# Attention statistics in PSUM, sums beside the values, and seven products in the second FFN throughout

## The chip, the cores and the metric

The kernel runs on one core of one Trainium2 chip. Its engines each work through an instruction queue of their own, in order: TensorE (PE; its weight loads are listed as PEld), VectorE (DVE), ScalarE (ACT), GpSimd (POOL) and SyncE (SP), which issues the DMAs. PE, DVE and ACT reach both on-chip memories, SBUF and PSUM; PE writes its results to PSUM, which is handled here as eight banks of 128 x 512 floats. The metric is the device time of one execution in microseconds (us). The profile is that of one execution.

## The reference

```python
xn = _layernorm(x)                                   # 2048 tokens x 512
qkv = xn @ wqkv                                      # 32 heads of 16
pq, pk = q @ w_phi, k @ w_phi                        # per head, 16 x 16
phi = concatenate([softmax(p), softmax(-p)])         # 32 features per head
kv = einsum("bhsf,bhsd->bhfd", phi_k, v)
z  = einsum("bhsf->bhf", phi_k)
num = einsum("bhqf,bhfd->bhqd", phi_q, kv)
den = einsum("bhqf,bhf->bhq", phi_q, z)[..., None] + 1e-6
s = (num / den).reshape(B, S, D) @ wo
act = mish(xn @ w1 + b1)                             # 1792 wide
g = silu(act @ w2)
return x + s * g
```

## The kernel before

Tokens are worked in 16 tiles of 128 (NT) or 4 groups of 512 (NG); the hidden width of 1792 is worked in 7 blocks of 256 (NB). A float32 factor is split in a high part (ACT rounds it) and a low part (DVE or POOL subtracts), and a product of two factors is three PE products, low x high, high x low, high x high. Most of the large products are of 128 x 128 weights with 512 columns.

Two by two block products are often done by seven products instead of eight (the schemes Ka to Kd for keys and values, Fa to Fd for the first FFN, Ga, Gb, Gc with Gd or Ge and Gf for the second). In the second FFN a unit is one group of 512 tokens and one block. Units of token groups 0 and 1 are plain (parts G0 to G13: 24 PE products each); groups 2 and 3 go as pairs by seven products (Ga7 to Ga13 and so on: 42 PE products for a pair and a block).

The attention runs in parts. K and Ka to Kd give keys and values; `k_soft` makes the features of a key tile: maximum and minimum per head, two subtractions to e, exponential on ACT, sum, reciprocal, scaling. `q_soft` (S) loads the projected queries qp, which had been written to DRAM as qd, and does the same without the scaling. `kv_acc` (A0 to A7) multiplies features with values into one PSUM bank, kvp, for two tiles at a time, and adds the features of all tokens in SBUF, zacc. `sums` (z) turns kvp and zacc into kvw, through DRAM, and the row sums zb, by four PE products pz with ones. `den` (D0 to D15) multiplies a query tile with zb (ez), sums to tz, takes the reciprocal, scales the tile and transposes it to ph. `num` (U) computes the numerators pn, `att_out` (O0 to O15) multiplies with wo (pw) and puts the result so in DRAM. `final` (E) reads it back, applies silu and adds x.

What runs where and when is set by three tables. ORDER lists the parts. SCHED lists every single operation of all parts in the order of issue, and for an operation that can go to two engines (`either`: DVE or POOL; `copy`: ACT or DVE) the letter behind the number (V, G, A) picks the engine. PLACE lists the buffer of each tile in its pool (slot, s2, sm, rq, st, tq, and ps for PSUM). Since queues run in order, an instruction that waits holds up all behind it on its engine.

All instructions of the loop are recorded by one helper, `call`, so their line is L184 in the profile; the names of the tiles tell them apart.

Of the kernel before, what the change touches and what calls it, by code (L numbers as in the profile page):

```python
# [37 lines left out]
Fa11 Fc10 Fc7 Fd10 D4 P5 P6 S5 Fd7 Fb11 Fc11 Fa13 D5 Fb13 Fa12 S7 S8 Fc13 Fb12 Fc12 Fd13 D8 D6 L2 S9 Fd11 Fa4 Fb4 S13
wo0 D7 Fd12 Fa5 Fc4 D9 Fa6 Fb6 Fc6 Fb5 Fd6 R0 Fc5 wo1 U1 Fd4 R2 Fd5 U0 G0 D10 O7 O4 O0 S11 D11 O3 S12 O2 D12 D13 S14
O6 O1 T0 R1 O5 B1 R3 G1 G2 G3 D14 R4 T1 R6 G4 R5 G5 G6 E3 Ga7 Ga8 S15 D15 G7 Ga9 E2 G8 T2 Ga10 E1 G9 E0 G10 G11 T4  # L40
Ga11 G12 G13 Ga12 Ga13 E7 E6 U3 Gb7 U2 Gb8 E5 O13 E4 O11 T3 Gb9 O8 Gb10 O14 B3 Gb11 O15 B0 B2 B4 Gb12 T6 B5 Gb13 O9 B6
E8 Gc7 O12 Gc8 Gc9 Gc10 Gc11 Gc12 Gc13 Ge7 Ge8 E9 Ge9 Ge10 O10 Ge11 Ge12 E14 E15 E12 E13 Ge13 Gf7 Gf8 E10 Gf9 Gf10
Gf11 Gf12 Gf13 E11
"""
SCHED = """
# [884 lines left out]
```

## Time and profile before

| | |
|---|---|
| median of 3 runs | 490.1 us (489.66 to 490.27) |
| span of the profiled execution | 488.0 us (its own time is not listed apart) |
| start of the first PE product | 1.1 us |
| end of the last PE product | 482.7 us |
| POOL, 128 x 1024 products ez of one tile | 2.4 us |
| DMAs on SP's queue, to and from HBM | 115.55 MB, mean 237 GB/s |

A row of a group reads: line, engine, operation, tile written <- tiles read, shapes, count | busy us, mean ns of one | idle time of the engine before them and what ended it. A row of waits reads: engine, tile, line <- what was waited for: us in total, times, longest. A row of the chain or of the timeline begins with start and length in us. PE's row lengths overlap, since products are pipelined; their cost in a stream is read from start to start or from the chain.

### The profile page before, as it was taken

The page shows a single profiled execution, that of the slowest core. Times are in us where ns is not written, and L with a number is a line of the kernel's source. Part 1 is how long each engine was busy: PE and PEld are TensorE (multiplying, and loading weights), DVE is VectorE, ACT ScalarE, POOL GpSimd, SP SyncE. Part 2 cuts the span into 40 slices and gives each one's busy share as a digit, 9 for nine tenths or more (in the row PEclk, how much of TensorE's full clock was granted, in tenths as well). Part 3 has the DMA queues.
Part 4 walks back from the last instruction along what each step waited for, and adds up shares of the span by engine and source line. Part 5 has one row for each costly group of instructions (what it writes and reads, how often), then busy time and mean ns, then how long its engine had stood idle before and what let it go on. Part 6 is the DMA issues. An engine that isn't in the chain of part 4 may idle for free.

```text
span 488.0 us, 8581 instructions
## 1 busy us (share of the span) xinstructions
PE 481.5 (99%) x3122; PEld 397.9 (82%) x3122; DVE 429.3 (88%) x687; ACT 284.6 (58%) x447; POOL 244.5 (50%) x188
## 2 busy tenths in 40 slices
PE   9999999999999999999999999999999999999995
PEld 9888888888888888888888878888888887888884
DVE  5989898899999997999999989998678588879984
ACT  5998777235154504325434676598976677576721
POOL 2675859967335786686557963312622032412021
PEclk9999999999999999999999999999999999999999
DMA  8956649165686789879969979788486615468543
GB/s 303 346 169 233 245 173 365 69 192 198 207 289 223 234 294 303 303 213 357 333 214 283 363 242 332 239 274 279 167 262 217 230 56 163 152 210 284 168 147 140
DMA packets 65594, 115.55 MB, mean 237 GB/s; under 512 B 7056, under 2 KB 32016, under 8 KB 65552
## 3 DMA queue, kind: packets, MB, share of 16 engines
q1 hardware_dynamic: 65408, 114.98, 69.9%
q8 instruction: 24, 0.39, 0.3%
q14 instruction: 18, 0.15, 0.1%
q10 hardware_dynamic: 144, 0.03, 0.0%
HBM read 72.92 MB, written 42.07 MB: 236 GB/s over the span
## 4 chain that ended last, share of the span: by engine, by line
PE 99%; DVE 0%; ACT 0%; DVEq 0%; issue 0%; ACTq 0%
PE y L184 20%; PE fx L184 16%; PE q L184 9%; PE pw L184 9%; PE kx L184 8%; PE x L184 8%; PE fy L184 8%; PE ky L184 4%; PE fz L184 4%; PE pn L184 2%; PE kz L184 2%; PE z L184 2%; PE kvp L184 2%; PE pt L184 1%; PE v L184 1%; PE k L184 1%
## 5 line engine op out<-in xcount | busy, mean ns | idle before, releaser
L184 PE MATMUL q<-wqh,xT 128*128 128x512 f32 x128 | 42.3, 393 | 0.0
L184 ACT ACTIVATE r<-r,b1t 128x512 f32<-128x512 f32 x56 | 38.1, 719 | 1.2 <-DMA r<-hd 1.1
L184 PEld LDWEIGHTS q<-wqh,xT 128*128 128x128 f32 x128 | 24.0, 188 | 5.0
L184 PE MATMUL q<-wql,xT 128*128 128x512 f32 x64 | 24.9, 390 | 0.0
L184 ACT ACTIVATE hc<-fx 128x512 f32<-128x512 f32 x11 | 6.5, 599 | 26.8 <-PE fx L184 15.9
L184 ACT ACT_TABLE_LOAD x16 | 20.5, 1283 | 0.3
L184 POOL TENSOR_TENSOR rs<-rs,mhalf 128x1 f32<-128x1 f32 x16 | 9.7, 615 | 19.7 <-DVE rs L184 19.7
L184 DVE TENSOR_REDUCE tz<-ez 128x64 f32<-128x1024 f32 x16 | 19.2, 1206 | 0.1
L184 PE MATMUL kx<-wss,th 128*128 128x512 f32 x56 | 17.3, 390 | 0.0
L184 POOL TENSOR_TENSOR tl<-ts,th 128x1024 fp32r<-128x1024 f32 x6 | 14.4, 2407 | 4.5 <-ACT th L184 3.1
L184 DVE TENSOR_TENSOR ol<-pn,oh 128x256 fp32r<-128x256 f32 x32 | 11.9, 416 | 5.1 <-ACT oh L184 5.1
L184 POOL TENSOR_TENSOR w1al<-w1a,w1ah 128x768 fp32r<-128x768 f32 x4 | 8.2, 2046 | 14.2 <-DVE w1sl L184 9.2
L184 POOL TENSOR_TENSOR w<-w2r,w 128x512 fp32r<-128x512 f32 x7 | 9.9, 1428 | 9.3 <-ACT w L184 9.3
L184 ACT ACTIVATE qs<-q 128x512 f32<-128x512 f32 x15 | 8.7, 594 | 9.4 <-PE q L184 5.0
L184 PEld LDWEIGHTS q<-wql,xT 128*128 128x128 f32 x64 | 12.0, 188 | 2.4
L184 ACT ACTIVATE oh<-pn 128x256 fp32r<-128x256 f32 x32 | 10.7, 393 | 4.9 <-PE pn L184 3.6
L184 POOL TENSOR_TENSOR w1s<-w1a 128x256 f32<-128x256 f32 x9 | 8.9, 995 | 7.4 <-PE q L184 7.1
L184 PE MATMUL pw<-oh,wo0l 128*128 128x512 f32 x32 | 12.4, 389 | 0.0
L184 PE MATMUL pw<-ol,wo0h 128*128 128x512 f32 x32 | 12.4, 389 | 0.0
L184 PE MATMUL pw<-oh,wo0h 128*128 128x512 f32 x32 | 12.4, 389 | 0.0
L184 PE MATMUL pw<-oh,wo1l 128*128 128x512 f32 x32 | 12.4, 389 | 0.0
L184 PE MATMUL pw<-ol,wo1h 128*128 128x512 f32 x32 | 12.4, 389 | 0.0
(869 smaller groups left out, 1833.1 us busy)
## 6 DMA issues: line engine op xcount, KB each, us to landing
r<-hd SPq DMA_DIRECT2D x28, 512.0 KB, 5.0
x<-x SPq DMA_DIRECT2D x16, 256.0 KB, 6.1
scr<-xT SPq DMA_DIRECT2D x8, 512.0 KB, 5.1
scrT<-th SPq DMA_DIRECT2D x8, 512.0 KB, 3.5
qd<-qs SPq DMA_DIRECT2D x16, 256.0 KB, 4.6
scrT<-tl SPq DMA_DIRECT2D x8, 512.0 KB, 4.8
qp<-qd SPq DMA_DIRECT2D x16, 256.0 KB, 5.1
xx<-xt SPq DMA_DIRECT2D x16, 256.0 KB, 4.9
```

What stands on the lines that cost most here:

```text
L184: getattr(g, m)(*a, **k)
```

## The change

- `softmax` keeps maximum, minimum, sum and (for keys) reciprocal in a PSUM bank `st` (tiles k0m, q0m and so on) of 6 x 32 columns instead of three SBUF tiles. Both subtractions and the scaling are fixed on DVE. The same holds for the small steps of `den`, all in a bank tz; the fused step (scalar_tensor_tensor) becomes a reduce and an addition of 1e-6.
- A value tile v has a last row of 16 ones (`v_tile`). `kv_acc` uses the values and these ones as weights' partner: the features e of a head are 32 weight columns, and the 16 values with the 16 ones are the 32 moving columns, so kvp holds the sums of keys times values and, beside them, the row sums. 32 products a tile instead of 16, each of 32 columns instead of 64. zacc, the ones_r products pz and the way of kvw through DRAM (5 DMAs) go.
- Queries are loaded by four DMAs of 64 KB a tile, in an order by which a plain 32 x 32 block transposition gives ph. `num` works on 4 tiles a time: 32 products of 512 columns instead of 64 of 256 (4 units as before), and the split of its result is 16 pairs of 512 columns instead of 32 of 256.
- The second FFN goes by seven products for all token groups; `ffn2` (the plain units) is gone. The pieces of w2 are loaded and split apart (`prep2`: R, `prep2d`: C, `prep2a`: T, `prep2b`: B, by `pair2`), for four blocks the sums of w2 lie in the pool tq.
- The final gate works in a PSUM bank, its two products fixed on DVE. b1 comes transposed from the host.
- ORDER, SCHED and PLACE are new throughout; the helper's line is L190.

Instructions before and after: PE matmul 2567 to 2649 (second FFN -42, numerators -128, kvp +256, pz -4); DVE tensor_tensor 383 to 407, reduce 112 to 128, tensor_scalar 63 to 81, scalar_tensor_tensor 16 to 0; POOL tensor_tensor 179 to 171; ACT activation 406 to 421; DMAs on SP 320 to 370.

```diff
+POOLS = dict(slot=SLOTS, s2=S2, tq=2, sm=13, rq=RQ, st=48, ps=8)
...
-Ga11 G12 G13 Ga12 Ga13 E7 E6 U3 Gb7 U2 Gb8 E5 O13 E4 O11 T3 Gb9 O8 Gb10 O14 B3 Gb11 O15 B0 B2 B4 Gb12 T6 B5 Gb13 O9 B6
+Gb2 O11 T3 Gb3 T4 Gb4 T5 O8 Gb5 T6 Gb6 B0 Gc0 O14 B1 Gc1 B2 Gc2 B3 Gc3 O15 B4 Gc4 B5
...
-    def softmax(p, name, r):
+    def softmax(p, name, r=None):
         p3 = p.rearrange("p (h d) -> p h d", d=DH)
-        mm = sm([P, 2, H], name + "m")
-        V.tensor_reduce(mm[:, 0, :], p3, axis=X, op=ALU.max)
-        V.tensor_reduce(mm[:, 1, :], p3, axis=X, op=ALU.min)
+        st = bank([P, 6, H], name + "m")
+        V.tensor_reduce(st[:, 0, :], p3, axis=X, op=ALU.max)
+        V.tensor_reduce(st[:, 1, :], p3, axis=X, op=ALU.min)
         e = slot([P, H, 2, DH], name + "e")
-        hi, lo = (mm[:, i, :, None].to_broadcast([P, H, DH]) for i in range(2))
-        either(e[:, :, 0, :], p3, hi, op=ALU.subtract)
-        either(e[:, :, 1, :], lo, p3, op=ALU.subtract)
+        hi, lo = (st[:, i, :, None].to_broadcast([P, H, DH]) for i in range(2))
+        V.tensor_tensor(e[:, :, 0, :], p3, hi, op=ALU.subtract)
+        V.tensor_tensor(e[:, :, 1, :], lo, p3, op=ALU.subtract)
         A.activation(e, e, AF.Exp)
-        s = sm([P, 2 * H], name + "s")
+        s = st[:, 2:4].rearrange("p a h -> p (a h)")
         V.tensor_reduce(s, e.rearrange("p h s d -> p (h s) d"), axis=X, op=ALU.add)
+        if r is None:
+            r = st[:, 4:6].rearrange("p a h -> p (a h)")
         V.reciprocal(r, s)
-        return e
+        return e, r
 
     def scale(e, r):
         e2 = e.rearrange("p h s d -> p (h s) d")
-        either(e2, e2, r[:, :, None].to_broadcast([P, 2 * H, DH]), op=ALU.mult)
-
-    kvp = bank([P, 4, 64], "kvp")
-    zacc = slot([P, 2 * D], "zacc")
+        V.tensor_tensor(e2, e2, r[:, :, None].to_broadcast([P, 2 * H, DH]), op=ALU.mult)
+
+    kvp = bank([P, 8, 32], "kvp")
...
+    def v_tile(t):
+        v = alloc("s2", [P, H + 1, DH], f"v{t}")
+        vp[t] = v
+        copy(v[:, H], ones[:, 0:DH])
+        return v[:, 0:H].rearrange("p h d -> p (h d)")
...
     def q_soft(t):
         p = s2(f"qp{t}")
-        Q.dma_start(p, qd[t])
+        for c in range(4):
+            Q.dma_start(p[32 * c:32 * c + 32, :].rearrange("p (b f) -> p b f", b=4),
+                        qd[t][:, c * P:(c + 1) * P].rearrange("(b p) f -> p b f", p=32))
         rq[t] = alloc("rq", [P, 2 * H], f"q{t}r")
-        eq[t] = softmax(p, f"q{t}", rq[t])
+        eq[t], _ = softmax(p, f"q{t}", rq[t])
 
     def kv_acc(p):
         ts = tile_of(p), tile_of(p) + 4
         es = [ek.pop(t) for t in ts]
         if p == 0:
             V.memset(kvp, 0.0)
-            either(zacc, *es, op=ALU.add)
-        else:
-            for e in es:
-                either(zacc, zacc, e, op=ALU.add)
         with one():
             for t, e in zip(ts, es):
                 v = vp.pop(t)
-                for i in range(H // 2):
-                    m = i % 4 * 32
-                    PE.matmul(kvp[m:m + 32, i // 4, :], v[:, i * 32:i * 32 + 32], e[:, i * 64:i * 64 + 64],
-                              start=False, stop=t == NT - 1, skip_group_check=True)
+                for j in range(8):
+                    for c in range(4):
+                        h = 8 * c + j
+                        PE.matmul(kvp[32 * c:32 * c + 32, j, :], e[:, h * 32:h * 32 + 32], v[:, h::H - h, :],
+                                  start=False, stop=t == NT - 1, skip_group_check=True)
 
 
     def den(t):
         ez = slot([P, H, 2, DH], f"ez{t}")
-        either(ez, eq[t], w["z"], op=ALU.mult)
-        tz = sm([P, 2 * H], f"tz{t}")
+        either(ez.rearrange("p (b h) s d -> p b (h s d)", b=4), eq[t].rearrange("p (b h) s d -> p b (h s d)", b=4),
+               w["z"][:, None, :].to_broadcast([P, 4, 2 * P]), op=ALU.mult)
+        st = bank([P, 6, H], f"tz{t}")
+        tz, dn, r2 = st[:, 0:2].rearrange("p a h -> p (a h)"), st[:, 2], st[:, 4:6].rearrange("p a h -> p (a h)")
         V.tensor_reduce(tz, ez.rearrange("p h s d -> p (h s) d"), axis=X, op=ALU.add)
         r = rq.pop(t)
-        dn = sm([P, H], f"den{t}")
-        either(tz, tz, r, op=ALU.mult)
-        tz3 = tz.rearrange("p (h s) -> p h s", s=2)
-        V.scalar_tensor_tensor(dn, tz3[:, :, 0], 1e-6, tz3[:, :, 1], op0=ALU.add, op1=ALU.add)
+        V.tensor_tensor(tz, tz, r, op=ALU.mult)
+        V.tensor_reduce(dn, tz.rearrange("p (h s) -> p h s", s=2), axis=X, op=ALU.add)
+        V.tensor_scalar(dn, dn, 1e-6, None, op0=ALU.add)
         V.reciprocal(dn, dn)
-        r3 = r.rearrange("p (h s) -> p h s", s=2)
-        either(r3, r3, dn[:, :, None].to_broadcast([P, H, 2]), op=ALU.mult)
-        scale(eq[t], r)
-
-        g, j = divmod(t, 8)
+        V.tensor_tensor(r2.rearrange("p (h s) -> p h s", s=2), r.rearrange("p (h s) -> p h s", s=2), dn[:, :, None].to_broadcast([P, H, 2]), op=ALU.mult)
+        scale(eq[t], r2)
+
+        g, j = divmod(t, 4)
         if g not in phT:
-            phT[g] = alloc("tq", [P, H, 8, 32], f"ph{g}")
-        V.transpose(phT[g][:, :, j, :], eq[t].rearrange("p h s d -> p h (s d)"))
-
-    def num(n):
...
+    def num(g):
+        ph = phT[g].rearrange("p t b h n -> p (t b) h n")
+        pn = [bank([P, D], f"pn{g}_{c}") for c in range(4)]
+        with one():
+            for a in range(2):
+                for m in range(4):
+                    for c in range(4):
+                        at = slice(32 * c, 32 * c + 32)
+                        PE.matmul(pn[c][32 * m:32 * m + 32, :], w["kvw"][at, m, a, :], ph[at, :, 2 * m + a, :],
+                                  start=a == 0, stop=a == 1, skip_group_check=True)
+        for i in range(2):
+            oT[g, i] = slot([P, 2, D], f"oh{g}_{i}", F32R), slot([P, 2, D], f"ol{g}_{i}", F32R)
+        for c in range(4):
+            split(pn[c], *(o[:, c % 2] for o in oT[g, c // 2]))
...
-    def ffn2(n):
...
-        u = h if h.space != "PSUM" else s2(f"u{n}")
+        u = h if h.space == "PSUM" else bank([P, D], f"u{n}")
         k = D // PIECES.get(n, 1)
         for i in range(0, D, k):
             c = slice(i, i + k)
             A.activation(u[:, c], h[:, c], AF.Silu)
-            either(u[:, c], u[:, c], st[:, c], op=ALU.mult)
-            either(xx[:, c], u[:, c], xx[:, c], op=ALU.add)
+            V.tensor_tensor(u[:, c], u[:, c], st[:, c], op=ALU.mult)
+            V.tensor_tensor(xx[:, c], u[:, c], xx[:, c], op=ALU.add)
...
     def sums():
-        kvf = slot([P, 4, 2, 2, DH], "kvf")
-        zt = slot([P, H, 2, DH], "zb")
-        zf = zt.rearrange("p h s d -> p (h s d)")
-        kvs, kvt = (alloc("s2", [P, 4 * 64], n) for n in ("kvs", "kvt"))
-        copy(kvs, kvp.rearrange("p c n -> p (c n)"))
-        V.transpose(kvt, kvs)
+        kz = alloc("s2", [P, 2, 2 * P], "kz")
+        kvf, zt = kz[:, 0].rearrange("p (g a b d) -> p g a b d", g=4, a=2, b=2), kz[:, 1]
+        zs = alloc("s2", [P, 8, 32], "zs")
+        copy(zs, kvp[:, :, DH:DH + 1].to_broadcast([P, 8, 32]))
+        V.transpose(zt, zs.rearrange("p h n -> p (h n)"))
         V.memset(kvf, 0.0)
         for a in range(2):
-            V.tensor_copy(kvf[:, :, a, a, :], kvt.rearrange("p (g a d) -> p g a d", g=4, a=2)[:, :, a, a * DH:a * DH + DH])
...
+            copy(kvf[:, :, a, a, :], kvp.rearrange("p (j a) n -> p j a n", a=2)[:, :, a, 0:DH])
+        w["z"], w["kvw"] = zt, kvf.rearrange("p j a b d -> p j a (b d)")
```

Keys times values on PE, the first group of A0. Before, four tiles in a row behind a product kx (rows: line, operation, tile written <- weights or values read, size, count):

```order
L184 MATMUL kx_417<-wss,tl_401 128x512
L184 MATMUL kx_417<-wss,th_400 128x512 x2
L184 MATMUL kvp<-k0e,v_214 32x64 x16
L184 MATMUL kvp<-k4e,v_272 32x64 x16
L184 MATMUL kvp<-k1e,v_347 32x64 x16
L184 MATMUL kvp<-k5e,v_321 32x64 x16
L184 MATMUL ky_457<-wss,tl_362 128x512
```

The same place of the changed kernel:

```order
L190 MATMUL kx_369<-wkl_158,xT_239 128x512
L190 MATMUL kx_369<-wkh_157,xT_239 128x512
L190 MATMUL kvp<-v_207,k0e 32x32 x32
L190 MATMUL kvp<-v_265,k4e 32x32 x32
L190 MATMUL pt_399<-ident,x_392 128x128 x4
L190 MATMUL kvp<-v_335,k1e 32x32 x32
L190 MATMUL kvp<-v_311,k5e 32x32 x32
L190 MATMUL pt_330<-ident,x_323 128x128 x4
L190 MATMUL kx_369<-wss_229,tl_256 128x512
```

Twice as many products of half the columns a tile, and transposes (pt) between the two groups.

Numerators on PE, the first unit; before, behind a product fx of the first FFN (the first rows of 64 products):

```order
L184 MATMUL fx_781<-ft3h_755,w1ah_686 128x512
L184 MATMUL pn_0_809<-ph_596,kvw 32x256
L184 MATMUL pn_1_810<-ph_596,kvw 32x256
L184 MATMUL pn_2_811<-ph_596,kvw 32x256
L184 MATMUL pn_3_812<-ph_596,kvw 32x256
```

Of the changed kernel (the first rows of 32):

```order
L190 MATMUL fx_698<-ft2h_689,w1sh_606 128x512
L190 MATMUL pn_0_736<-ph_547,kz 32x512
L190 MATMUL pn_1_737<-ph_547,kz 32x512
L190 MATMUL pn_2_738<-ph_547,kz 32x512
L190 MATMUL pn_3_739<-ph_547,kz 32x512
```

Half as many products, of twice the columns; the weights kz now come straight from SBUF.

The denominators on DVE, in the middle of `den` of the first tiles. Before:

```order
L184 TENSOR_TENSOR hb_559<-hb_559,fy_558 128x512
L184 COPY ha_630<-fx_628 128x512
L184 TENSOR_REDUCE tz_612<-ez_611 128x64
L184 TENSOR_REDUCE tz_637<-ez_636 128x64
L184 SCALAR_TENSOR_TENSOR den_613<-tz_612 128x32
L184 TENSOR_TENSOR ez_646<-q3e,zb 128x1024
L184 TENSOR_TENSOR ha_630<-ha_630,fz_629 128x512
L184 RECIPROCAL q2r<-q2s 128x64
L184 TENSOR_TENSOR q4e<-qp_619,q4m 128x32x16
```

After:

```order
L190 TENSOR_REDUCE tz_594<-ez_593 128x64
L190 RECIPROCAL q4r<-q4m 128x64
L190 TENSOR_SCALAR tz_546<-tz_546 128x32
L190 TENSOR_TENSOR tz_594<-tz_594,q3r 128x64
L190 TENSOR_REDUCE tz_594<-tz_594 128x32
L190 TENSOR_SCALAR tz_594<-tz_594 128x32
L190 RECIPROCAL tz_594<-tz_594 128x32
L190 TENSOR_TENSOR q1e<-q1m,qp_494 128x32x16
L190 TENSOR_REDUCE q1m<-qp_494 128x32
L190 TENSOR_TENSOR q1e<-qp_494,q1m 128x32x16
```

The steps of one denominator stand directly behind one another, in a PSUM bank, and the subtractions q1e that POOL could take stand on DVE beside them.

More of the change, by code (lines that the diff above doesn't have):

```diff
@@ L256, in block_kernel @@
     ones = const.tile([P, P], F32, name="ones")
-    ones_r = const.tile([P, P], F32R, name="ones_r")
     mhalf = const.tile([P, 1], F32, name="mhalf")
@@ L267, in block_kernel @@
     nc.vector.memset(mhalf, -0.5)
-    nc.scalar.activation(ones_r, ones, AF.Copy)
     wake = bank([P, P], "wake")
@@ L544, in num @@
[L544 to L562 removed]
+            phT[g] = alloc("tq", [P, 4, 4, 8, 32], f"ph{g}")
@@ L591, in prep1, with pair2, prep2, prep2d @@
         w1_[b] = ts
+    def pair2(b, n, src):
+        m = src.shape[1]
+        if n == 3 and b < 4:
+            if b == 0:
+                w2_["tq"] = alloc("tq", [P, 4, 2, 2, 2 * P], "w2sb", F32R)
+            t = w2_["tq"][:, b]
+        elif n == 1:
+            if b % 2 == 0:
+                w2_["c"] = slot([P, 2, 2, 1, 2 * P], f"w2x{b}_1", F32R)
+            t = w2_["c"][:, b % 2]
+        else:
+            t = slot([P, 2, m, 2 * P], f"w2x{b}_{n}", F32R)
+        split(src, t[:, 0], t[:, 1], either)
+        w2_[b, n] = t
+    def prep2(b):
+        a = alloc("s2", [P, 2, 2 * P], f"w2r{b}")
+        Q.dma_start(a, w2[b][:, 0:2])
+        pair2(b, 0, a)
+    def prep2d(b):
+        a = alloc("s2", [P, 1, 2 * P], f"w2c{b}")
+        Q.dma_start(a, w2[b][:, 3:4])
+        pair2(b, 1, a)
     def load_w2(b, name):
@@ L596, in load_w2 @@
         return a
-    def split_w2(src, name, t=None):
-        t = slot([P, 2, 2, 2 * P], name, F32R) if t is None else t
-        split(src, t[:, 0], t[:, 1], either)
-        return t
-    def prep2(b):
-        a = load_w2(b, "w2r")
-        w2_[b] = [split_w2(a[:, 2 * e:2 * e + 2], f"w2{e}_{b}") for e in range(2)]
     def prep2a(b):
@@ L708, in load_m @@
         return r
-    def ffn2(n):
-        g, b = divmod(n, NB)
-        ah, al = split_raw(load_m(g, b), f"a{n}")
-        for e in range(4):
-            if b == 0:
-                hs[4 * g + e] = bank([P, D], f"y{4 * g + e}")
-            wt, c = w2_[b][e // 2], slice(e % 2 * P, (e % 2 + 1) * P)
-            with one():
-                for f in range(2):
-                    mm3(hs[4 * g + e], (wt[:, 0, f, c], wt[:, 1, f, c]), (ah[:, f], al[:, f]), b == 0 and f == 0, b == NB - 1 and f == 1)
     def product2(ps, wt, i, ah, al, first, last):
@@ L755, in ffn2b @@
             yb[q] = banks(f"y{q}_")
[L756 to L758 removed]
+        last, wt = b == NB - 1, w2_[b, 2]
+        product2(yb[q], wt, 1, ah[:, 1], al[:, 1], b == 0, last)
+        product2(xb[q], wt, 0, ah[:, 0], al[:, 0], False, last)
         if last:
@@ L779, in ffn2d @@
         last = b == NB - 1
-        product2(xb[q], w2_[b][1], 1, hl[:, 0], hl[:, 1], False, last)
+        product2(xb[q], w2_[b, 1], 0, hl[:, 0], hl[:, 1], False, last)
         if last:
@@ L856, in bias @@
     def bias():
[L857 removed]
+        Q.dma_start(b1t, b1)
     def sums():
[L860 to L865 removed]
+        kz = alloc("s2", [P, 2, 2 * P], "kz")
[3 more added lines that the diff above has]
+        V.transpose(zt, zs.rearrange("p h n -> p (h n)"))
         V.memset(kvf, 0.0)
         for a in range(2):
[L868 to L882 removed]
+            copy(kvf[:, :, a, a, :], kvp.rearrange("p (j a) n -> p j a n", a=2)[:, :, a, 0:DH])
+        w["z"], w["kvw"] = zt, kvf.rearrange("p j a b d -> p j a (b d)")
     wqT = [None] * KC
```

267 lines of the change are left out of this document (116 added, 151 removed), and 40 rows, old and new, of the table PLACE.

## Prediction

> **What bounds the kernel now.** I read the page's busy line and its chain of waits first, then the waits of TensorE (PE), then VectorE (DVE) by stretches of the span.
>
> ```profile
> span 488.0 us, 8581 instructions
> PE 481.5 (99%) x3122; PEld 397.9 (82%) x3122; DVE 429.3 (88%) x687; ACT 284.6 (58%) x447; POOL 244.5 (50%) x188
> ...
> PE 99%; DVE 0%; ACT 0%; DVEq 0%; issue 0%; ACTq 0%
> ...
> PE wake L184 <- DVE mhalf L267: 1.1, 1, 1.1
> ```
>
> The chain is PE for 99% of the span, and PE's one listed wait is the first 1.1 us. So a product that goes shortens the run by its own length, as long as every other engine still delivers ahead of PE. DVE at 88% is the engine that could fail to. Its stretches (columns: span, then busy time of PE, weight loads, DVE, ACT, POOL, then granted clock, DMA share and rate):
>
> ```profile
> 0.00:335.00 335.00, 333.81 (x2241) 277.22 (x2242) 309.03 (x515) 185.90 (x302) 207.86 (x161) 1.00 0.76 259
> 335.00:488.00 153.00, 147.71 (x883) 120.64 (x881) 120.31 (x174) 98.73 (x145) 36.64 (x27) 1.00 0.57 188
> ```
>
> Up to 335 us, DVE is idle for only 335.0 - 309.0 = 26.0 us. After that it idles for 33. The granted clock is 1.00 throughout. Half of the early idle time isn't spare either; these are the first and last of ten rows in which DVE waited for PE itself, 10.5 us in all, and two others:
>
> ```profile
> DVE ha L184 <- PE fz L184: 1.8, 2, 1.0
> ...
> DVE ha L184 <- PE fx L184: 0.3, 1, 0.3
> ...
> DVE phit L184 <- DMA phic<-phi: 2.7, 1, 2.7
> DVE ol L184 <- ACT oh L184: 2.4, 3, 1.3
> ```
>
> So 26.0 - 10.5 = 15.5 us of DVE's idle time there was forced by other engines and DMAs.
>
> **PE, term by term.** Chain rows (start, length, what), then rows of the timeline:
>
> ```profile
> 113.60 1.92 PE kvp L184 x128
> 115.53 1.58 PE ky L184 x6
> ...
> 275.24 1.36 PE fx L184 x6
> ...
> 280.68 2.68 PE pn L184 x117
> ...
> 323.21 28.56 PE y L184 x126
> ```
> ```profile
> 113.53 0.65 PE L184 MATMUL kvp<-k0e,v 128*32 128x64 f32 x32
> 114.00 0.63 PE L184 MATMUL kvp<-k4e,v 128*32 128x64 f32 x32
> ...
> 280.61 2.75 PE L184 MATMUL pn<-ph,kvw 32*32 32x256 f32 x128
> ...
> 60.81 1.03 PE L184 MATMUL pt<-ident,x 128*128 128x128 f32 x8
> ```
>
> *Second FFN.* A product of 512 columns costs 28.56/126 = 0.2267 us. Units 0 and 1 took 24 products each per block, 48 together; by seven products the pair takes 42. Over 7 blocks 42 products go: -9.5 us.
>
> *Row sums.* The four 512-column products pz that summed zacc go: -0.9 us.
>
> *Keys times values.* A tile takes 0.45 us (113.53 to 114.00, then 0.45 and 0.44) with 32 trace records, so 15.0 ns each for 128 records in 1.92 us. Four records stand side by side on four column groups: 60 ns a quad, of which the stream of 64 columns, twice, is 2 x 64 x 0.2267/512 = 57 ns. All 512 records are 7.6 us now. The change makes 1024 of half the columns. If the stream still sets the pace the total stays (+0). If 15 ns is a price per record, it doubles (+7.6). For weight loads there is one row to go by: transposes load 128 columns each and start 0.109 us apart (8 in 1.03 us with a last one of about 0.27), so 32 columns load in some 27 ns, the same as the halved stream, if the four column groups load side by side as the quads now show. I take +1.0, near the stream's end.
>
> [...]
>
> *Numerators.* A unit takes 2.68 us for 128 records of 256 columns, sixteen side by side. The stream alone would be 8 rounds of 0.2267, which is 1.81. The excess is 0.87, or 6.8 ns per record. The change has as many units but 64 records of 512 columns each: stream 1.81, excess from 0 to 0.87. Halving it with the records gives 2.25, so 4 x 0.43 = -1.7 us (bounds 0 and -3.5).
>
> *Mode changes.* Six products behind kvp took 1.58 instead of 1.36, so a change between the small and the full array costs 0.2 us. The order has kvp in more places, with transposes between: +0.4.
>
> Sum for PE: -9.5 - 0.9 + 1.0 - 1.7 + 0.4 = **-10.7 us**.
>
> **DVE.** Here the change both adds and removes much.
>
> ```profile
> 48.40 1.21 DVE L184 TENSOR_REDUCE k1s<-k1e 128x64 f32<-128x1024 f32 x1
> 49.65 0.55 DVE L184 RECIPROCAL k1r<-k1s 128x64 f32<-128x64 f32 x1
> 50.12 0.10 DVE L184 TENSOR_SCALAR mv<-st 128x1 f32<-128x1 f32 x1
> ...
> L184 DVE TENSOR_TENSOR ol<-pn,oh 128x256 fp32r<-128x256 f32 x32 | 11.9, 416 | 5.1 <-ACT oh L184 5.1
> L184 DVE TENSOR_TENSOR kp<-kp,kz 128x512 f32<-128x512 f32 x7 | 4.8, 685 | 1.6 <-PE kz L184 1.6
> L184 DVE SCALAR_TENSOR_TENSOR den<-tz 128x32 f32<-128x32 f32 x16 | 5.1, 325 | 0.3 <-POOL tz L184 0.2
> L184 DVE TENSOR_TENSOR w2s<-w2s 128x256 f32<-128x256 f32 x8 | 3.2, 416 | 0.0
> L184 DVE TENSOR_TENSOR zacc<-zacc,k6e 128x1024 f32<-128x1024 f32 x1 | 1.2, 1226 | 0.0
> L184 DVE TENSOR_TENSOR k12e<-kp,k12m 128x512 f32<-128x512 f32 x1 | 1.6, 1551 | 0.0
> ...
> L184 POOL TENSOR_TENSOR q0e<-qp,q0m 128x512 f32<-128x512 f32 x1 | 2.0, 2042 | 0.0
> L184 POOL TENSOR_TENSOR k6e<-k6e,k6r 128x1024 f32<-128x1024 f32 x1 | 2.0, 1961 | 0.0
> ```
>
> The first three rows show how DVE rows add up. The scalar operation starts 0.08 before its predecessor ends; the reciprocal needs the row just before it and starts 0.04 after that ends. So an instruction costs its row less 0.08, and a pair in direct dependence costs 0.12 more.
>
> Added: 46 subtractions of 512 elements that POOL did (at 2.04 us) at 0.68 - 0.08 = 0.6, with the measured mix 25.7; 15 scalings of 1024 that POOL did (at 1.96) at 1.14, with the measured mix 16.3; the denominator's small steps in place of the fused one, 1.2. Together +43.2. Removed: 11 row sums zacc and zaccl, -13.0; 6 of 8 products ez, which go to POOL, -7.1; and the splits of the plain units (13 of 1024 elements, -15.3), several weight splits and copies, less the sums that seven products need, together -23.4. The balance is -0.3. But the order raises directly dependent pairs from 43 to 109: 66 x 0.117 = **+7.7 us**. DVE ends near 437 us busy.
>
> Against PE: a statistics bank is one of the eight PSUM banks, so the PE product that gets it next waits until the chain on it is through, and all of PE's queue waits behind that product. The tightest late place is the product pw of output tile O11, 335 us into PE's rows: it takes the bank of query tile 15 and waits for that tile's reciprocal. The DVE rows up to this reciprocal add up to 319.6 us at the durations above (an estimate). With PE's start at 1.1 us, DVE may idle for 16.6 us before PE has to stop; 15.5 were forced before. That is a margin of 1.1, where it was 10.5. Some waits will miss it, so I add a stall of **+2 us** (0 when all fit, 9.4 when DVE idles for 26.0 as before). Behind 335 us the margin grows; PE's remaining rows stand 17 to 40 us behind DVE's.
>
> **PSUM for statistics.** Some 320 DVE instructions (7 per key tile, 6 per query tile, 7 per denominator) now read or write PSUM. The rows: a 256-element subtraction with one operand in PSUM takes 416 ns (ol), with both in SBUF 416 ns (w2s). I take 0. A gain is possible, too: k12e, with both operands in SBUF, once took 1551 ns where its kind takes 685. With a PSUM operand I count nothing for that.
>
> [...]
>
> **At no cost.** ACT (58%) takes a little more, POOL (50%) loses the subtractions and scalings and takes ez and weight splits; DVE and PE are the cover. SP issues 50 more DMAs, among them 48 more for the query tiles, with rows of 512 bytes where they had 2 KB; the DMA share up to 335 us is 0.76, and no wait on query data stands among DVE's. Were that cover gone, the query subtractions would be late and fall under the stall bound. The round trip of the key-value sums through DRAM goes; PE had other products beside it and didn't wait for it, so no time comes back. The tail (5.3 us after PE) has the same pieces: 0.
>
> **Sum.** The profiled span is 488.0 us, the median of the runs 490.1, so 2.1 lie around it and stay. 490.1 - 10.7 + 2.0 = **481.4 us**.
>
> **Rivals.**
> - *B, price per record.* If kvp keeps 15 ns per record, add 6.6: **488.0**. For: PE's records have other small prices (6.8 ns in pn). Against: 57 of 60 ns in a quad are the stream. Chance 0.11.
> - *F, a floor per record.* If so short a product costs what a record of pn costs (2.68/128 = 20.9 ns), 1024 take 21.4 us, +13.8 instead of +1.0: **494.2**, slower. Against: 15.0 is measured in the same product. Chance 0.03. [...]
> - *C, DVE sets the pace up to 335 us.* It idles for 26.0 as before where 16.6 are free: stall 9.4 instead of 2, **488.8**. For: the margin of 1.1. Against: 10.5 of the 26.0 were waits for PE, which shrink when PE is no longer ahead. Chance 0.16.
> - *D, slower.* Place: the chains of reduce, subtract, reciprocal and multiply on PSUM banks, 320 instructions, nearly all ahead of the 335 us mark. If none of them overlapped its predecessor, the 254 that aren't among the 66 new pairs would lose 0.083 each, 21 us; less the margin of 1.1, PE stalls for 20: 479.4 + 20 = **499.4**. It decides for slower from (10.7 + 1.1)/254 = 46 ns each. For: statistics written into PSUM aren't in the trace, nor operations with both operands there. Against: 416 and 416. Chance 0.10. [...]
> - *E, the small products gain more.* kvp at the stream, numerators without excess, no stall: -1.0 - 1.8 - 2.0, **476.6**. Chance 0.07.
> - *A, forecast,* stalls of 0 to 4 us: 479 to 484. Chance 0.53. That the second FFN doesn't get shorter is excluded by the count of products.
>
> **How the numbers follow.** A and E are faster (0.60); of B and C about seven in ten are (0.19), with the rest at or above 489. A difference of 0.2% (1 us) is about what a measurement can tell. D and F are slower (0.13). Faster 0.79, same 0.05, slower 0.16. The range takes in E and its unknown, A, B and most of C, and leaves out D and F: 475 to 490.
>
> **What would show it.** Right: PE still over 98% of the chain; kvp rows under 0.55 us a tile; pn near 2.2 us a unit; no y of plain units; DVE near 437 us with PSUM subtractions at 0.68; PE's waits under 4 us in sum, most of them for DVE before 335 us. Wrong: kvp at 0.9 a tile (B); PE waiting for e, tz or ph chains for 8 us and more (C); PSUM subtractions or reciprocals that start 40 ns later behind their predecessor than now (D). Outside all of them lies a DMA-bound stretch, above all with the query tiles' small rows.

## The result and the profile after

The changed kernel is slower: 505.01 us median of 4 runs (501.67 to 508.44), against 490.19 (489.66 to 490.28) for the kernel before, measured beside it. The ratio is 1.0303 [1.0257, 1.0350]. The forecast was 481.4 in a range of 475 to 490, so it was wrong in size and in sign. The profiled run took 501.67 us, with a span of 499.9; it is the fastest of the four.

The page of the changed kernel: span, busy times, granted clock in 40 slices, a DMA queue (transfers, MB, share), and the shares of the chain:

```profile
span 499.9 us, 9100 instructions
PE 480.2 (96%) x3332; PEld 390.8 (78%) x3332; DVE 445.0 (89%) x728; ACT 291.3 (58%) x459; POOL 254.7 (51%) x180
PEclk9999998999998989999999999999999999999999
q8 instruction: 26, 0.43, 0.4%
PE 77%; DVE 6%; POOL 5%; issue 4%; ACT 3%; DMA 3%; SPq 0%; DVEq 0%; POOLq 0%
```

PE was 99% of the chain and is now 77%. PE's busy time fell by only 1.3 us, though 42 products of the second FFN alone should have taken 9.5 out. And there is a releaser that the page before had at 0%: "issue", in which an engine waits for nothing that the profile shows. The clock has three slices at 8. PE's waits (in total, times, longest):

```profile
PE kvp L190 <- issue: 11.5, 4, 4.9
PE wake L190 <- DVE mhalf L272: 1.1, 1, 1.1
PE x L190 <- DVE mb12l L190: 0.6, 1, 0.6
PE kx L190 <- DVE mv L190: 0.3, 1, 0.3
PE x L190 <- DVE h L190: 0.2, 1, 0.2
PE ky L190 <- DVE v L190: 0.2, 1, 0.2
```

One wait of 11.5 us, in four pieces, in front of the products of keys times values, and for no engine. The timeline of PE shows the first piece (start, length, operation, tiles, shapes, records merged, idle time before):

```profile
79.98 0.73 PE L190 MATMUL kvp<-v,k0e 128*32 128x32 f32 x62
...
80.56 0.74 PE L190 MATMUL kvp<-v,k4e 128*32 128x32 f32 x62
...
81.82 0.73 PE L190 MATMUL kvp<-v,k1e 128*32 128x32 f32 x62
...
82.40 0.21 PE L190 MATMUL kvp<-v,k5e 128*32 128x32 f32 x2
85.17 1.07 PE L190 MATMUL kvp<-v,k5e 128*32 128x32 f32 x60 [2.55 <-issue]
```

From k0e to k4e it is 0.58 us, and k1e takes as much: some 9 ns for each of 64 records. That is the stream that the forecast assumed. But the fourth tile stops after four of its 64 records (two are in rows left out) and goes on 2.55 us later. Its operands were there, since the same tile was already under way, and the profile names no engine that it waited for. The 60 records behind the stall then take 1.0 us instead of 0.5. The stretches around the four stalls show why: TensorE's granted clock is down (columns: span, busy times, granted clock, DMA share, rate):

```profile
82.00:89.00 7.00, 4.45 (x139) 3.88 (x129) 5.24 (x9) 1.06 (x1) 0.00 (x0) 0.76 0.10 33
112.50:119.50 7.00, 5.50 (x113) 4.56 (x101) 6.68 (x11) 3.37 (x6) 2.16 (x2) 1.00 0.49 171
153.00:161.00 8.00, 4.45 (x75) 3.78 (x76) 4.00 (x7) 0.77 (x2) 0.00 (x0) 0.79 0.85 297
180.00:188.00 8.00, 5.52 (x59) 4.33 (x48) 4.91 (x9) 1.54 (x2) 0.85 (x1) 0.79 0.85 273
```

Behind three of the four stalls the clock falls to half for 3.41 us each (a mean of 0.76 to 0.79 over the stretch), so 3 x 1.7 = some 5 us more are lost. Behind the shortest, of 1.5 us, it doesn't.

Where the time went on PE is best seen from start to start: each product is charged with the time until the next one starts, and the sums are grouped by the tile it writes (worked out from all PE records of the two profiled runs, in us):

| tile | before | after | difference |
|---|---|---|---|
| kvp, keys times values | 7.56 | 22.82 | +15.3 |
| kx, ky, keys and values | 58.13 | 60.99 | +2.9 |
| fx, fy, fz, first FFN | 133.97 | 136.08 | +2.1 |
| pt, transposes | 6.18 | 7.46 | +1.3 |
| second FFN (x, y, z) | 143.15 | 135.52 | -7.6 |
| pn, numerators | 10.74 | 9.13 | -1.6 |
| pz, row sums | 0.94 | 0 | -0.9 |
| last PE start in the span | 482.32 | 493.56 | +11.2 |

Behind the last PE start come 6.3 us, where it was 5.7. So what the change was to save on PE did come, for the most part (-10.1). It is more than eaten by kvp.

### The profile page after: what moved, and what is told of

It reads as the page before. It is cut to its first block, busy times and chain, and to the rows that moved or that the text cites. A ratio compares the mean times of both kernels' runs of the same rounds, so it can differ in the third digit from the quotient of the medians.

```text
span 499.9 us, 9100 instructions
## 1 busy us (share of the span) xinstructions
PE 480.2 (96%) x3332; PEld 390.8 (78%) x3332; DVE 445.0 (89%) x728; ACT 291.3 (58%) x459; POOL 254.7 (51%) x180
## 4 chain that ended last, share of the span: by engine, by line
PE 77%; DVE 6%; POOL 5%; issue 4%; ACT 3%; DMA 3%; SPq 0%; DVEq 0%; POOLq 0%
PE fx L190 16%; PE x L190 13%; PE fy L190 8%; PE pw L190 7%; PE q L190 5%; PE y L190 5%; PE kx L190 5%; PE fz L190 4%; PE z L190 4%; PE ky L190 2%; PE kvp L190 2%; PE pn L190 2%; POOL wss L190 1%; DMA scrT<-th 1%; PE kz L190 1%
## 5 line engine op out<-in xcount | busy, mean ns | idle before, releaser
L190 PE MATMUL q<-wqh,xT 128*128 128x512 f32 x128 | 42.3, 391 | 0.0
L190 ACT ACTIVATE r<-r,b1t 128x512 f32<-128x512 f32 x56 | 37.9, 713 | 2.0 <-DMA r<-hd 1.9
L190 POOL TENSOR_TENSOR tl<-ts,th 128x1024 fp32r<-128x1024 f32 x7 | 16.9, 2411 | 26.6 <-ACT th L190 26.5
L190 PEld LDWEIGHTS q<-wqh,xT 128*128 128x128 f32 x128 | 24.0, 188 | 5.1
L190 POOL TENSOR_TENSOR w1sl<-w1s,w1sh 128x1024 fp32r<-128x1024 f32 x7 | 16.8, 2401 | 20.2 <-PE kx L190 13.0
L190 PE MATMUL q<-wql,xT 128*128 128x512 f32 x64 | 25.0, 390 | 0.0
L190 POOL TENSOR_TENSOR rs<-rs,mhalf 128x1 f32<-128x1 f32 x16 | 10.3, 664 | 23.0 <-DVE rs L190 20.1
L190 POOL TENSOR_TENSOR w1al<-w1a,w1ah 128x768 fp32r<-128x768 f32 x7 | 13.0, 1853 | 17.7 <-ACT w1ah L190 11.9
L190 POOL TENSOR_TENSOR t<-r,mt 128x512 f32<-128x512 f32 x8 | 10.4, 1299 | 20.2 <-issue 9.4
L190 DVE TENSOR_REDUCE tz<-ez 128x64 f32<-128x1024 f32 x16 | 19.2, 1204 | 0.7 <-POOL ez L190 0.2
L190 ACT ACTIVATE hc<-fx 128x512 f32<-128x512 f32 x14 | 8.0, 596 | 18.3 <-PE fx L190 18.3
L190 PE MATMUL kx<-wss,th 128*128 128x512 f32 x56 | 18.4, 411 | 0.0
L190 ACT ACTIVATE hb<-fx 128x512 f32<-128x512 f32 x10 | 6.0, 598 | 20.5 <-PE fx L190 12.0
L190 ACT ACTIVATE v<-kx 128x512 f32<-128x512 f32 x14 | 8.3, 596 | 15.9 <-PE kx L190 15.9
L190 ACT ACTIVATE ha<-fx 128x512 f32<-128x512 f32 x12 | 7.2, 596 | 17.2 <-PE fx L190 17.2
L190 POOL TENSOR_TENSOR mt<-r,r 128x512 f32<-128x512 f32 x9 | 13.4, 1492 | 7.3 <-ACT r L190 7.2
L190 ACT ACTIVATE hd<-fx 128x512 f32<-128x512 f32 x10 | 5.9, 596 | 17.8 <-PE fx L190 13.2
L190 ACT ACTIVATE u<-h 128x512 f32<-128x512 f32 x12 | 7.1, 598 | 13.4 <-DVE h L190 13.4
L190 ACT ACTIVATE kp<-kx 128x512 f32<-128x512 f32 x11 | 6.5, 595 | 12.9 <-PE kx L190 11.6
L190 PEld LDWEIGHTS q<-wql,xT 128*128 128x128 f32 x64 | 12.0, 188 | 2.5
L190 PEld LDWEIGHTS kx<-wss,th 128*128 128x128 f32 x56 | 11.4, 204 | 2.5
```

Of the source, the lines that this page charges most:

```text
L190: getattr(g, m)(*a, **k)
```

## The theory, and the experiments

**Theory S, supply.** The profile has a DMA queue q8 of the kind "instruction", with transfers of 16384 bytes each. By the theory it brings PE's own instructions, in blocks of 256. The numbers fit: the page counts 3122 products and as many weight loads before, 6244 / 256 = 24.4, and 24 such transfers; after, 6664 / 256 = 26.0, and 26.

```profile
q8 instruction: 24, 0.39, 0.3%
```

(That is the row of the page before.) A group of four key tiles was 256 PE instructions and is now 512, in some 2.3 us with the transposes between. If PE holds only about two blocks (an estimate from the 496 to 533 instructions counted below), it runs dry: the next block comes too late for instructions as short as these. Counted over all PE instructions in the trace, semaphore and drain instructions included (6730 in all), the four stalls of the changed kernel begin behind number 1217, 1985, 2753 and 3521. All four are 193 modulo 256, so by the theory PE stops where one block ends and the next begins, at a block's edge. Up to the stalls 496 to 533 instructions ran since the last finished transfer began; elsewhere the transfers follow each other after 64 to 382 instructions, where long products run mostly after 210 to 260.

The times of the transfers show the cause more directly than the counts do (worked out from the DMA records of q8 and all PE records of the ten profiled runs). In the changed kernel, the transfers at the four stalls begin at 82.62, 111.81, 154.20 and 180.47 us, and PE goes on 2.54, 2.63, 2.24 and 2.21 us later. Counting the stops of the experiments below as well, there are 23 at such an edge, and each ends 2.2 to 2.8 us after its transfer began. At all other edges that have a transfer on record, PE arrives 2.97 us or more after it began, and waits for no instruction. So in these runs PE stops when it reaches an edge before its block is there. In the changed kernel the four transfers begin 0.9 to 4.1 us after PE passed the edge before, and 256 of these short instructions take some 1.15 us.

**Rivals.** R1: a price per record, as in B and F of the prediction, that shows only in some places. R2: contention for the PSUM bank kvp, or the form of the product (features as weights, values as columns). R3: statistics in PSUM and a busier DVE (C, D) set the time, and the stalls only fall on slack. In the expectations below, "rival D" is not the D of the prediction but another one: the products wait for late features or values. "Rival V" is R3, the vector engine or any other part of the change.

**1. Spread.** The same products, but the tiles are issued one by one: from start to start 2.3 to 20 us apart in the trace, all but the last two (tiles 11 and 15), which still stand side by side, 0.6 us apart. An operation of the table may be named by halves:

```diff
         for s in SCHED.split():
+            s, _, part = s.partition("/")
             i = int(s.rstrip("VGA"))
-            left.remove(i)
+            left.discard(i)
             op = self.ops[i]
+            if part:
+                n = len(op["PE"]) // 2
+                op = {"PE": op["PE"][int(part) * n:int(part) * n + n]}
```

> The changed kernel, with the 16 tiles' keys-times-values products issued one tile at a time, 3 to 15 us of other products between (as far as the buffers allow), instead of two or four tiles in a row. Theory S (supply: PE runs through the instructions of four tiles, 512 records of products and weight loads, faster than new ones are fetched): the stalls inside kvp, 11.5 us in the profile, go to under 3 us, with them the stretches of half clock behind them (3 x 3.4 us at half speed, 5 us lost), less 2 us for more changes between array modes; time 505 to about 488 (485 to 492). Rival D (data: the products wait for late features or values): the same tiles are as late, so PE waits 8 us or more in front of them, time 498 to 506. Rival V (the vector engine or another part of the change sets the time): 500 to 506.

Measured: 491.71 us (490.86 to 492.61), ratio to before 1.0039 [1.0024, 1.0054]. PE's waits:

```profile
PE pt L195 <- DVE x L195: 1.5, 1, 1.5
PE kvp L195 <- issue: 1.4, 1, 1.4
```

The granted clock is 1.00 in every stretch up to 480 us. The 13 us go with the row of short products; the same 1024 records on the same bank are there. R1 and R2 fall. The stall that is left lies inside tile 15, behind instruction 3521, in the one pair that still stands together. kvp costs 14.2 us here, not 7.6, because it now stands at 15 places: 14.2 less the stream (16 x 0.57 = 9.1) and the 1.4 of waiting leaves 3.7, an estimated 0.25 us for each of 15 changes to small products and back.

**2. The kernel before, with halved products.** Each product of 64 columns is done as two of 32, with nothing else changed: no statistics in PSUM, no new order, the old form of the product.

```diff
-                for i in range(H // 2):
+                for n in range(H):
+                    i, u = n // 8 * 4 + n % 4, n // 4 % 2 * 32
                     m = i % 4 * 32
-                    PE.matmul(kvp[m:m + 32, i // 4, :], v[:, i * 32:i * 32 + 32], e[:, i * 64:i * 64 + 64],
+                    PE.matmul(kvp[m:m + 32, i // 4, u:u + 32], v[:, i * 32:i * 32 + 32], e[:, i * 64 + u:i * 64 + u + 32],
```

> The kernel before, with each keys-times-values product of 64 columns issued as two of 32 columns: same data, same places, twice the instructions. Theory S: PE stalls of 2 to 5 us inside each group of four or more tiles, stretches of half clock behind them; time 490 to 502 to 515. Rival D and rival V: nothing but the products themselves changes, so at most 2 us more: 490 to 493. Price per record (15 ns each): 498, with kvp rows at twice their length and no gaps.

Measured: 516.24 us (515.72 to 517.12), ratio 1.0541 [1.0526, 1.0557]; clock 0.974. PE's waits:

```profile
PE kvp L184 <- issue: 16.8, 5, 5.6
```

One edit of the product's length makes the old kernel 26 us slower, 1 us more than the top of theory S's range and far outside the others'. Its stalls begin behind PE instruction 1473, 2241, 2497, 3265 and 3521, all 193 modulo 256 again, and there are 28 transfers on q8 for 7268 instructions. None of the other parts of the change is needed for such a loss.

**3. Half the heads.** The changed kernel with every second j left out, so half the heads get no sums: rows of 256 instructions as before.

```diff
-                for j in range(8):
+                for j in range(0, 8, 2):
```

> The changed kernel with half of the keys-times-values products left out (every second j, so half of the heads have no sums): four tiles are 256 records of products and weight loads again, as in the kernel before. Theory S: no stall inside kvp, no half clock; time about 484 (480 to 488). Rival D: the remaining products wait for the same tiles: 499 to 505. Rival V: 500 to 505.

Measured: 485.26 us (484.73 to 486.32), ratio 0.9910 [0.9894, 0.9925]. No stall for issue; what is left among PE's waits:

```profile
PE fx L190 <- DVE ha L190: 1.3, 1, 1.3
...
PE pt L190 <- DVE x L190: 0.6, 1, 0.6
PE x L190 <- DVE mb12l L190: 0.5, 1, 0.5
PE fx L190 <- DVE hb L190: 0.5, 1, 0.5
```

This run also weighs the rest of the forecast. kvp takes 6.2 us here. With the 8.6 that the forecast had for it, the time would be 485.3 + 2.4 = 487.7, not 481.4. So some 6 us are missing besides the stalls. This kernel leaves half of the sums out, so it is no candidate.

**4. Twice the stream.** Each product streams its 32 columns twice, into 64 columns of the bank; as many instructions, each twice as long.

```diff
-    kvp = bank([P, 8, 32], "kvp")
+    kvp2 = bank([P, 8, 2, 32], "kvp")
+    kvp = kvp2[:, :, 0]
...
-                        PE.matmul(kvp[32 * c:32 * c + 32, j, :], e[:, h * 32:h * 32 + 32], v[:, h::H - h, :],
+                        PE.matmul(kvp2[32 * c:32 * c + 32, j], e[:, h * 32:h * 32 + 32], v[:, None, h::H - h, :].to_broadcast([P, 2, 2, DH]),
```

> The changed kernel with each keys-times-values product streaming its 32 columns twice into 64 columns of PSUM (the second half isn't used): as many instructions, twice the stream, so a tile lasts 1.0 us and not 0.56. Theory S: while PE streams longer, the fetch has more time; the stalls shrink by about the 7 us that the stream adds, to 4 to 6 us; time about 500 (495 to 505), no longer than the changed kernel although its products take 7 us more. Rival D and rival V: the products' 7 us are added: 509 to 513.

Measured: 501.49 us (499.65 to 505.05), ratio 1.0241 [1.0186, 1.0296].

```profile
PE kvp L190 <- issue: 8.9, 4, 4.1
```

Twice the stream costs no time: a tile takes 0.91 us from start to start instead of 0.57, some 5.4 us more in all, and the time is not above the changed kernel's 501.67 to 508.44. If records or columns set the pace here, the time would have risen. The stalls begin at the same four counts, but they shrank less than theory S said: to 8.9 us, where 4 to 6 were expected. Much of the rest is the clock, with one stretch of 3.41 us at half clock in this profile where the changed kernel's had three.

**5. Pairs apart.** A part A stays in one piece (two tiles, 256 instructions), and the eight parts are moved apart by their places in SCHED. In the trace they start 7 to 28 us apart, but the last one only 4.7 us behind the one before it.

> The changed kernel with the two tiles of each part A still in a row, but the eight parts kept apart by 5 us or more of other products where the buffers allow. Theory S: a part is 256 instructions of PE, one of the blocks in which they are fetched, and the products behind it give the fetch its time: no stall or one short one; eight changes of array mode instead of sixteen save about 2.5 us against the tiles one by one (491.7): 488 (486 to 490), at or below the kernel before. Rival D: as with the tiles one by one or longer: 492 to 503.

Measured: 493.52 us (492.03 to 495.24), ratio 1.0074 [1.0057, 1.0091]. Theory S's range is missed by 3.5 us, and by its time alone this lies in rival D's. PE's waits, and a stretch around the last stall, are those of S (the profiled run is the slowest of the six, 495.24 us):

```profile
PE kvp L194 <- issue: 2.3, 2, 2.2
PE fy L194 <- DVE hb L194: 1.3, 1, 1.3
...
PE pt L194 <- DVE x L194: 0.7, 1, 0.7
PE kx L194 <- DVE k5e L194: 0.7, 1, 0.7
```
```profile
171.00:180.00 9.00, 6.83 (x146) 5.42 (x145) 5.94 (x10) 2.62 (x5) 1.09 (x1) 0.81 0.79 253
```

4.7 us from one part's start to the next aren't enough: at 172 us, behind instruction 3521 and inside tile 15, PE still stops for 2.2 us, and later runs at half clock for 3.41. The transfer of that block began only 4.1 us after PE had passed the edge before.

**6. Shifted.** 32 tiny products (128 PE instructions with their parts and weight loads) are added to the warm-up. If the stalls hang on blocks, their counts stay and other tiles are hit.

```diff
-    for _ in range(WAKE):
+    for _ in range(WAKE - 1):
         PE.matmul(wake, ones, ones, start=True, stop=True)
+    with one():
+        PE.matmul(wake, ones, ones, start=True, stop=True)
+        for _ in range(32):
+            PE.matmul(wake[0:32, 0:8], ones[:, 0:32], ones[:, 0:8], start=True, stop=True)
```

> The changed kernel with 32 tiny products (32 x 8) at the end of the warm-up, which move all later instructions of PE by 128 places. Theory S: instructions come in blocks at fixed places of the stream, so the stalls stay at the same count of PE instructions from the start (about 1217, 1985, 2753, 3521) and so hit one tile (128 instructions) earlier: in the first group inside or right behind k1's products instead of k5's. Rival D: the stalls stay in front of the same products (k5, k7, k13, k15), 128 counts later.

Measured (one run): 504.98 us.

```profile
PE kvp L190 <- issue: 9.4, 4, 4.3
PE kx L190 <- ACT k3e L190: 2.0, 1, 2.0
```

The four stalls begin behind 1217, 1985, 3009 and 3521, again all 193 modulo 256, and they now cut k1e, k3e, k13e and k11e, where they had cut k5e, k7e, k13e and k15e. One more stop, of 2.0 us, begins behind 1473, at the same remainder; the profile names ACT's k3e for it, which had ended 0.5 us before PE went on, while the block's transfer had begun 2.6 us before, as at the other stops. The first stall shrank to 0.5 us, and the third came one block later than in the changed kernel. So the block's edge decides where PE can stop, not the tile, and rival D falls. How long it stops depends on when the transfer begins, and that the theory doesn't foretell.

**7. Statistics in SBUF.** Experiment 5 with the statistics st and tz in four SBUF buffers instead of PSUM banks, everything else in the same order. This undoes the part of the change that rival D of the prediction was about.

```diff
+    def stat(name):
+        next(places)
+        return pools["sx"].tile([P, 6, H], F32, tag="sx%d" % STAT[name], name=name)
...
-        st = bank([P, 6, H], name + "m")
+        st = stat(name + "m")
...
-        st = bank([P, 6, H], f"tz{t}")
+        st = stat(f"tz{t}")
```

> The kernel with the parts A kept apart, and its statistics in SBUF buffers again instead of PSUM banks (same engines, same order). If PSUM costs nothing for them: within 1.5 us of the kernel with the parts apart, small DVE rows as long as there. [...] If two SBUF operands make DVE and POOL get into each other's way: DVE subtractions of 1.2 to 1.6 us in place of 0.68 beside POOL's rows, and 2 to 6 us slower.

Measured: 543.72 us (540.90 to 547.79), ratio to before 1.1117 [1.1075, 1.1159], so 50 us above experiment 5. The last of the expectations has DVE and POOL in each other's way, as the rows below show them, but with 2 to 6 us; 50 was expected by none. DVE's busy time is the place, 493.8 us instead of 443.9; POOL's rises too, from 254.7 to 276.0:

```profile
PE 493.5 (91%) x3332; PEld 393.6 (73%) x3332; DVE 493.8 (91%) x728; ACT 291.7 (54%) x459; POOL 276.0 (51%) x180
```

A group of DVE in experiment 5, and the same in experiment 7 (count: shortest, median, longest in ns):

```profile
L194 DVE TENSOR_SCALAR tz<-tz x16: 170/192/200, 183.5 to 356.1; 128x32 f32<-128x32 f32 x16
```
```profile
L195 DVE TENSOR_SCALAR tz<-tz x16: 117/181/2383, 198.7 to 402.2; 128x32 f32<-128x32 f32 x16
```

The median even falls a little, but single ones take 2.4 us. The timeline of DVE and POOL shows such a moment:

```profile
222.43 0.21 DVE L195 TENSOR_TENSOR tz<-q3r,tz 128x64 f32<-128x64 f32 x1
222.68 1.23 DVE L195 TENSOR_TENSOR q3e<-q3e,tz 128x1024 f32<-128x1024 f32 x1
223.82 2.43 DVE L195 TENSOR_TENSOR tz<-q0r,tz 128x64 f32<-128x64 f32 x1
226.28 2.21 DVE L195 TENSOR_TENSOR q0e<-q0e,tz 128x1024 f32<-128x1024 f32 x1
...
222.69 3.48 POOL L195 TENSOR_TENSOR ez<-q1e,kz 128x1024 f32<-128x1024 f32 x1 [7.29 <-DVE tz L195]
226.13 1.29 POOL L195 TENSOR_TENSOR w2t<-w2t 128x512 f32<-128x512 f32 x1
```

The DVE product q0r by tz, 0.2 us by itself, ends at 226.25, as POOL's ez does at 226.17, and the next ends 1.1 us behind POOL's w2t. ez takes 3.48 where POOL's took 2.39 to 2.48 in the changed kernel. These rows, with their operands in SBUF, look as if the two engines went one after the other; what makes them do so isn't shown by any run. Here the price is 50 us of DVE time. In the groups that read a statistic beside another tile or itself, the extra time adds up to some 50 us (the two subtractions of keys and queries +25.7, the steps of tz +22.5, the scaling of keys +4.3, summed over the records).

**8. The last part later.** Experiment 5 with A7 moved further back, so that it starts 8.3 us behind the part before it instead of 4.7, and the two steps that read kvp behind it. The line of SCHED that changes:

```diff
-698A 878 677 684 696 918 917 920 685 713 791 686 729 1031 858 867 919 734 818 819 777 736 827V 735 828 792 793A 921 748
+698A 878 677 684 696 918 917 920 685 713 791 686 729 1031 858 867 919 734 818 819 736 735 792 793A 921 748 777 827V 828
```

> The kernel with the eight parts A kept apart, its last part (tiles 11 and 15) 2.7 us later still, with the steps that read its sums behind it: 8 us from the start of the part ahead, where it was 5. Theory S: the last stall inside kvp (2.4 us) and the half clock behind it (1.7 us) go: 493.5 to about 489.5 (488 to 491), level with the kernel before; what is then missing to the forecast of 481.4 is PE waiting for DVE (about 5 us) and changes of array mode (3 us). Rival D: the stall stays in front of tile 15: 492 to 496.

Measured: 492.06 us (491.61 to 492.71), ratio 1.0046 [1.0032, 1.0059]. Clock 0.999.

```profile
PE fx L194 <- DVE ha L194: 1.3, 1, 1.3
...
PE kvp L194 <- issue: 1.0, 1, 1.0
PE pt L194 <- DVE x L194: 0.7, 1, 0.7
PE kx L194 <- DVE k5e L194: 0.7, 1, 0.7
PE x L194 <- DVE mb12l L194: 0.6, 1, 0.6
```

The stall in tile 15 and the slow clock are gone, as S said, but another stop of 1.0 us is left, in tile 14 behind instruction 3265. The time falls by 1.5 us only, where 4 were expected: S's range ends at 491, and 492.06 is the low end of rival D's. Part of that miss is that the 4 were read from experiment 5's slowest run; between the two profiled runs (495.24 and 491.61) the difference is 3.6. With the supply mostly mended the changed kernel is still 0.46% above the kernel before. No version that ran computes all of the reference and beats the kernel before.

## Why the prediction was wrong, point by point

**The step that failed: "Keys times values".** It asked what a record costs in the stream, weighed 0, +1.0 and +7.6, and took "+1.0, near the stream's end". As a price of the stream that was right: 16 tiles at 0.56 to 0.58 us are 9.1, and the loss came from elsewhere. What it left out, by theory S, is that a record also has to be fetched. The group of four tiles grew from 256 to 512 PE instructions, and in the profiled run PE stood still for 11.5 us at the edges of blocks and ran three times 3.41 us at half clock, which cost some 5 us more. Where +1.0 us was forecast for kvp, +15.3 was measured. Experiments 1 and 2 show it from both sides: spread the same products and 13.3 us go; halve the products of the old kernel and 26 us come. That the supply comes in blocks of 256 rests on the places of the stalls, all 193 modulo 256, and on 24, 26 and 28 transfers for 6244, 6664 and 7268 instructions. How many instructions PE can hold isn't shown; in the changed kernel it ran dry 496 to 533 after the last finished transfer began.

**Rivals B and F** had a price per record in mind (7.6 or 13.8 in all). They were nearer to the time by accident: kvp at 22.8 looks like a floor of 22 ns per record, but the rows between stalls give 9. Experiment 4 tells these apart.

**The stall of +2 us for DVE, "margin of 1.1", was too small.** In experiment 3, with no stall for issue, the time is some 6 us above what its sum would give. From start to start, as in the table above, that run has +3.6 in the first FFN, +1.6 in keys and values and +0.9 in transposes, its second FFN saved 7.6 instead of 9.5, and its tail is 0.7 longer: 8.7 us together, where the sum had 2.0 for stalls and 0.4 for mode changes, which leaves 6.3. Of the 8.7, PE's listed waits for DVE are 3.4 (1.3, 0.6, 0.5, 0.5, 0.3 and 0.2). So C had the right direction, a DVE that is late more often than the margin said. How the rest divides between changes from small to full products and waits too short to be listed isn't settled.

**DVE: nearly right.** 437 was forecast, 445.0 measured. DVE's work before 335 us:

```profile
0.00:335.00 335.00, 321.98 (x2535) 264.06 (x2536) 303.03 (x540) 175.62 (x295) 169.37 (x128) 0.98 0.75 253
335.00:500.00 165.00, 158.19 (x799) 126.70 (x797) 141.96 (x189) 115.69 (x166) 85.30 (x53) 0.99 0.54 177
```

DVE now idles 32 us up to there, where it was 26.0. Its listed waits for PE are 11.5 us of that, where they were 10.5; its other listed waits are for ACT, DMA and POOL.

**PSUM for statistics, taken at 0: right as a price, wrong as a value.** The operations on one key tile:

```profile
L190 DVE TENSOR_TENSOR k12e<-kp,k12m x1: 678/678/678, 120.2 to 120.2; 128x512 f32<-128x512 f32 x1
L190 DVE TENSOR_TENSOR k12e<-k12m,kp x1: 685/685/685, 120.8 to 120.8; 128x512 f32<-128x512 f32 x1
...
L190 DVE RECIPROCAL k12m<-k12m x1: 567/567/567, 129.3 to 129.3; 128x64 f32<-128x64 f32 x1
L190 DVE TENSOR_TENSOR k12e<-k12e,k12m x1: 1224/1224/1224, 129.9 to 129.9; 128x1024 f32<-128x1024 f32 x1
```

678 and 685 ns with a PSUM operand, where the same subtraction of another tile (k14e) took 685 before with both in SBUF: no extra time for the operand in PSUM appeared. Nor did the sign of rival D, rows that start 40 ns later: a reciprocal directly behind its sum starts 0.034 us after that sum ends (median), where it was 0.035. So the kernel became slower, as D had it, but not by D's mechanism. The odd row of 1551 ns that the prediction quoted and set aside was the important one: it ran from 116.21 to 117.77 us beside POOL's second subtraction of the same tile, which ended at 117.22, so it too looks like DVE held up by POOL. In this order the PSUM operand keeps 50 us of such waiting away (experiment 7).

**Right:** the numerators (2.25 a unit forecast; 2.29 and 2.28 in the chain, -1.6 in the table against -1.7), the row sums (-0.9), and the tail within 0.7 us.

```profile
299.57 2.29 PE pn L190 x61
...
306.16 2.28 PE pn L190 x62
```

**Its other signs.** PE was to stay over 98% of the chain (77%), with waits under 4 us in sum (13.9) and kvp rows under 0.55 us a tile (0.56 to 0.58 between stalls).

**Still open:** why the runs of the changed kernel differ by 7 us where those of the kernel before differ by 0.6. The granted clock would account for most of it: the four runs took 501.67, 504.88, 505.14 and 508.44 us at a mean clock of 0.988, 0.983, 0.980 and 0.977, and 0.011 of some 500 us is an estimated 5.5 us. So the slower runs had more time at a lowered clock, but only the first has a trace that shows behind which stops. Also open is why a transfer begins late, which decides how long PE stops. Fetches that queue behind other DMAs would do it, but the four stretches don't bear it out: with a DMA share of 0.10, 0.49, 0.85 and 0.85 the transfers begin 2.0, 0.9, 4.1 and 1.6 us after PE passed the edge before. Experiment 7 used its own assignment of the four buffers, so its 50 us hold for this order alone.

## What to carry to other kernels

Count PE's instructions per microsecond, weight loads too, and not only its columns: here PE waited 11.5 us for "issue" with 512 in a group at 4 to 5 ns each, 2.3 with 256 in a row (experiment 5), and 1.4 with tiles of 128, spread out but for one pair (experiment 1). The kernel before, with half as many products of twice the length in rows of up to 384, had no such stall. Where an engine that has its operands waits for "issue", compare the places of the waits, counted in instructions, and the times of the instruction queue's transfers, before looking for a data hazard: 22 of the 23 stops here were listed so, and each ended 2.2 to 2.8 us after a transfer began. When a kernel mixes DVE and POOL work, look at DVE groups whose longest row is far above their median (here 2383 against 181 ns): in experiment 7 a row of 2430 ns ended 0.08 us behind POOL's ez, and with the operand in PSUM (experiment 5) the longest of that group was 200 ns.

## What the hardware showed that was not expected

- PE's stops in rows of short products began at 193 modulo 256 of its count of traced instructions, in the changed kernel and in experiments 1, 2 and 4 to 8. Each ended 2.2 to 2.8 us after a transfer of 16384 bytes began on the queue q8, of the kind "instruction".
- Stalls of 2.2 us and more in the changed kernel and in experiments 2, 4, 5 and 6 were followed by a stretch at half clock of 3.41 us or a multiple of it; those of 1.0 to 2.0 us in the changed kernel and in experiments 1, 4, 6 and 8 were not. The length alone doesn't decide: in experiment 7, PE stood still for 2.5 us at 71 us and the granted clock stayed at 1.00, while 1.9 us at 179 us were followed by 3.41 us at half clock. So 1.9 us of idle time were enough there, and 2.5 were not.
- Four products side by side on column groups start some 9 ns apart per record when each streams 32 columns, weight loads included (the changed kernel, from k0e to k4e: 0.58 us for 64 records).
- Single DVE operations with all operands in SBUF stretched from 0.21 to 2.43 us beside one POOL operation, ez (experiment 7).
